# Rest tile in two units, paired partial sums and a new order of side tiles in a fused attention and feed-forward kernel

## The chip, the cores and the metric

One core of a Trainium2 chip. The metric is the device time of one execution in microseconds (us). Runs agree within 0.3%; all are fast, with a granted TensorE clock of 0.996 to 1.0.

## The reference

For each of four batches a set of 32 inducing rows attends to the 12416 tokens (phase 1, giving h), the tokens attend to h (phase 2), and a gated feed-forward layer follows.

```python
B, N, m, C = (4, 12416, 32, 128)          # n_tokens 49664, d_ff 1536
def mab(q, kv):
    s = scale * (q @ kv.transpose(0, 2, 1))
    a = np.exp(s - s.max(-1, keepdims=True))
    a /= a.sum(-1, keepdims=True) + 1e-09
    return a @ kv
h = mab(I, x)                              # phase 1: m x C per batch
x = mab(x, h)                              # phase 2
gate = np.maximum(x @ w_gate, 0.0); val = x @ w_val
out = gate * val @ w_out
```

## The kernel before

The product h x w_gate, h x w_val (called hgv) is made once per batch, so that gate and value of a token block come from matmuls of 32 rows. A batch has 97 tiles of 128 tokens: 12 pairs of 512-token blocks and one **rest tile**. A pair is 12 **units**, one for each 128 of the 1536 columns. The main loop takes one unit per **slot**:

```python
for k, ps in enumerate(unit["g"]):        # ScalarE: relu of two banks, one unit
    nc.scalar.activation(out=g16[:, k * BLK : (k + 1) * BLK], in_=ps, func=AF.Relu)
for a in range(0, n, w):                  # VectorE: gate * value, of an earlier unit
    nc.vector.tensor_tensor(out=ready["dst"][:, a : a + w],
        in0=ready["g16"][:, a : a + w], in1=ready["v"][:, a : a + w], op=ALU.mult)
```

Twelve output matmuls (a **chain**, six slots) sum a block in the one bank of kind "o"; ScalarE copies it out as oT. PSUM has three banks "g" (gates and all side work), two double banks "v" and one "o". Everything else is a **side tile**, put into a slot by a list of (first slot, last slot): the scores of phase 2 (p2, p2q), phase 1 of the next batch (p1T, the h parts with their copies hp and hq, z, hT), and hgv. A side tile is taken in the fifth slot of a chain:

```python
due = [f for f in fills if f[0] <= at]
late = min(due, key=lambda f: f[1])
if late[1] <= at:
    pick = late                            # its deadline is here: forced
elif not n_steps or job_slot == 5:
    pick = due[0]                          # the one that could start first
```

The rest tile was three units of 512 columns, in one gate bank each, and an h part summed 4 groups of tiles in one bank, seven times per batch:

```python
for s in range(3):
    yield dict(mm=[[(slice(i * P, (i + 1) * P), 4 * s + i, p2[r : r + 32, 0:P], hgv[r : r + 32, :])
                    for i in range(4)] for r in (0, 64)], ...)
def h_part(at, q):
    ps = bank("g", "h_ps", [P, P + 1])
    ...                                    # 4 + 16 matmuls of one part
    nc.scalar.copy(out=hq[0:n, :], in_=ps[0:n, :])
    nc.gpsimd.tensor_tensor(out=s["hp"][0:n, :], in0=s["hp"][0:n, :], in1=hq[0:n, :], op=ALU.add)
```

The softmax here doesn't subtract the row's maximum and nothing guards it: scores larger than these inputs give would overflow.

Of the kernel before, what the change touches and what calls it, by code (L numbers as in the profile page):

```python
# [18 lines left out]
def kernel(  # L19
# [16 lines left out]
    nc = tc.nc  # L36
# [302 lines left out]
    count = itertools.count()  # L339


    SPB = NPAIR * NFF + 3


    def slot(b, pr, s):
        if b == B - 1 and pr >= NPAIR - 1:
            return b * SPB + (NPAIR - 1) * NFF + (3 if pr < NPAIR else 0) + s
        return b * SPB + pr * NFF + s

    def order(b):  # L350
# [112 lines left out]
    for b in range(B):  # L463
        for qd in range(NPAIR // 2):
            base = slot(b, 2 * qd, 0)
            if base:

                a = base - 2 * NFF if qd else slot(b - 1, NPAIR, 0) - 14
                if b == B - 1 and qd == NPAIR // 2 - 1:

                    bl = 2 * NPAIR - 4
                    ev_s2(b, (b, 2 * qd), (bl, bl + 1, bl, bl + 1), a + 4, a + 8)
                    for k in range(2):
                        ev_s2(b, (b, 2 * qd + 1, k), (bl + 2 + k,) * 4, a + 16 + 6 * k, a + 20 + 6 * k)
                else:
                    ev_s2_quad(b, qd, a + (4 if a else 12), a + (8 if a else 18))
            else:
                ev_s2(b, (b, 1), (2, 3, 2, 3), 7, 8)
                ev_z2(lambda: p2s[(0, 0)], [(0, 0, k) for k in range(2)], TPB, 2)
        a = slot(b, NPAIR, 0)  # L480
        ev_s2_rest(b, a - 11, a - 4)


    def plan_phase1(b):
        s = state[b] = {}
        at0 = slot(b - 1, 0, 0)

        def begin():
            s["x16"] = new_x16()
# [4 lines left out]
        for q in range(NCH):  # L494
            t0, t1 = crange(q)

            def load(q=q):
                s["x32", q] = load_x(b, q)

            def cast(q=q, t0=t0, t1=t1):  # L500
                nc.gpsimd.tensor_copy(  # L501
                    out=s["x16"][:, t0:t1, :], in_=s["x32", q]
                )

            def transp(q=q, t0=t0, t1=t1):
                s["xT"][q] = new_xT(q)
                nc.sync.dma_start_transpose(
                    out=s["xT"][q],
                    in_=s["x16"][:, t0:t1, :].rearrange("p t c -> p (t c)"),
                )  # L510

            at = at0 + 14 * q if q < NQ else at0 + 7
            post[at + 3].append(load)
            post[at + 11].append(cast)
            post[at + 15].append(transp)

            def s1(at, q=q):
                fill(at + 9, at + 24, lambda at: h_part(at, q))
                ps = bank("g", "s1T_ps")
                for r in range(4):  # L520
                    t = q * CT + r * TPB
                    nc.tensor.matmul(
                        ps[32 * r : 32 * r + 32, :],
                        indT,
                        xTs(s["xT"], t, TPB),
                        start=True,
                        stop=True,
                    )

                def act():  # L530
                    p1T = st([P, BLK], FP16, "p1T", 3)
                    nc.scalar.activation(out=p1T, in_=ps, func=AF.Exp, scale=sm_scale)  # L532

                    def tr():
                        p1g = st([P, TPB, P], FP16, "p1g", NQ)
                        nc.sync.dma_start_transpose(out=p1g, in_=p1T)
                        s["p1g"][q] = p1g

                    post[at + 2].append(tr)

                post[at + 1].append(act)

            if q < NQ:
                fill(at + 22, at + 34, s1)

        at = at0 + 34

        def s1_rest(at):
            fill(at + 12, at + 24, lambda at: h_part(at, NQ))
            ps = bank("g", "s1T_ps")  # L550
            nc.tensor.matmul(ps[0:M, 0:P], indT, xTs(s["xT"], NT - 1, 1), start=True, stop=True)

            def act():
                p1T = st([P, BLK], FP16, "p1T", 3)
                nc.scalar.activation(
                    out=p1T[0:M, 0:P], in_=ps[0:M, 0:P], func=AF.Exp, scale=sm_scale
                )

                def tr():
                    p1r = st([P, 1, M], FP16, "p1r", 1)  # L560
                    nc.sync.dma_start_transpose(out=p1r, in_=p1T[0:M, 0:P])
                    s["p1r"] = p1r

                post[at + 2].append(tr)

            post[at + 1].append(act)

        fill(at, at + 6, s1_rest)

        def h_part(at, q):  # L570
            ps = bank("g", "h_ps", [P, P + 1])
            if q < NQ:
                n = P
                for t in range(TPB):
                    nc.tensor.matmul(
                        ps[:, P : P + 1],
                        s["p1g"][q][:, t, :],
                        ones16[:, 0:1],
                        start=(t == 0),
                        stop=(t == TPB - 1),  # L580
                    )
                for t in range(TPB):
                    for r in range(4):
                        nc.tensor.matmul(
                            ps[32 * r : 32 * r + 32, 0:P],
                            s["p1g"][q][:, t, 32 * r : 32 * r + 32],
                            s["x16"][:, q * CT + r * TPB + t, :],
                            start=(t == 0),
                            stop=(t == TPB - 1),
                        )  # L590
            else:
                n = M
                p1r = s["p1r"][:, 0, :]
                nc.tensor.matmul(ps[0:M, P : P + 1], p1r, ones16[:, 0:1], start=True, stop=True)
                nc.tensor.matmul(
                    ps[0:M, 0:P], p1r, s["x16"][:, NT - 1, :], start=True, stop=True
                )

            def act():
                if "hp" not in s:  # L600
# [1 line left out]
                    nc.scalar.copy(out=s["hp"], in_=ps)  # L602
                    return
                hq = st([P, P + 1], FP32, "hq", 2)
                nc.scalar.copy(out=hq[0:n, :], in_=ps[0:n, :])  # L605
                nc.gpsimd.tensor_tensor(  # L606
                    out=s["hp"][0:n, :], in0=s["hp"][0:n, :], in1=hq[0:n, :], op=ALU.add
                )
                if q == NQ - 1:
                    fill(at + 3, at + 8, z_join)  # L610

            post[at + 1].append(act)

# [1 line left out]
        def z_join(at):  # L615
# [16 lines left out]
                )  # L632

            post[at + 1].append(act)
            fill(at + 4, at + 8, h_join)

        def h_join(at):
            ps = bank("g", "hT_ps", [P, M])
# [2 lines left out]
            def act():  # L641
# [2 lines left out]
                    nc.scalar.copy(out=s["hT"][:, d * M : (d + 1) * M], in_=ps)  # L644
                s["hgv"] = new_hgv()
                for k in range(3):
                    ev_hgv(b, k, at + 2, at + 9 + 3 * k)

            post[at + 1].append(act)

# [4 lines left out]
    def chain(w, gv, key, k, t0, first):  # L655
# [46 lines left out]
            if key[0] == B - 1 and key[1] == NPAIR - 2:  # L702
                counts = (6, 5) if k == 0 else (4, 4)
        else:
            steps = [(first + i // 4, lambda i=i: step(i)) for i in range(NFF)]
            counts = ([4, 8], [4, 8])
        job(steps, evac, counts)

# [69 lines left out]
    def units():  # L778
        for b in range(B):
            for pr in order(b):  # L780
# [67 lines left out]
                else:  # L848
                    gvr = st([P, NFF, P], FP16, "gvr", 1)
                    chain(P, lambda i, g=gvr: g[:, i, :], (b, pr), 0, NT - 1, base + 4)  # L850
                    for s in range(3):
                        yield dict(
                            mm=[
                                [
                                    (
                                        slice(i * P, (i + 1) * P),
                                        4 * s + i,
                                        p2[r : r + 32, 0:P],
                                        hgv[r : r + 32, :],
                                    )  # L860
                                    for i in range(4)
                                ]
                                for r in (0, 64)
                            ],
                            dst=gvr[:, 4 * s : 4 * s + 4, :].rearrange("p i c -> p (i c)"),
                        )

    def form(ps, cols, s, p2, hgv):
# [1 line left out]

    def gate_banks(unit):

        n = unit["dst"].shape[-1] // BLK
        unit["g"] = [None] * n

        def gate(cols, s, p2, hgv):
            k, lo = divmod(cols.start, BLK)
# [19 lines left out]
    while True:  # L897
# [42 lines left out]
        if due:  # L940
            late = min(due, key=lambda f: f[1])
            if late[1] <= at:
                pick = late
            elif not n_steps or job_slot == 5:
                pick = due[0]
        if pick and n_steps > 1 and isinstance(c, int):
            if len(j["steps"]) - n_steps + 1 <= 3 * (c - job_slot):
                n_steps -= 1
# [13 lines left out]

        if unit:
            g16 = unit["g16"] = st([P, 2 * BLK], FP16, "g16", 4)
            for k, ps in enumerate(unit["g"]):
                nc.scalar.activation(out=g16[:, k * BLK : (k + 1) * BLK], in_=ps, func=AF.Relu)  # L966
        if ready:
            n = ready["dst"].shape[-1]
            w = n // ready.get("parts", 1)
            for a in range(0, n, w):  # L970
                nc.vector.tensor_tensor(  # L971
                    out=ready["dst"][:, a : a + w],
                    in0=ready["g16"][:, a : a + w],
                    in1=ready["v"][:, a : a + w],
                    op=ALU.mult,
                )
        at += 1

# [29 lines left out]
```

## Time and profile before

| | before |
|---|---|
| time, median | 708.68 us (708.39 to 709.48, 4 runs) |
| span of the profiled run | 706.6 us |
| VectorE, ScalarE, TensorE busy | 677.7, 676.1, 637.6 us |
| first multiplication begins, last one ends | 26.81, 702.56 us |
| multiplications' distances above the minimum | 16.6 us |
| TensorE's waits for oT at a chain's first matmul | 45.7 us, 94 times |

The multiplications' distances above the minimum are worked out from the single VectorE starts of the trace: the distance from one multiplication's start to the next, less 1.131 us for 1024 columns, 0.617 for 512, which are the shortest usual distances.

In the profile's lines, L971 is line 971 of the kernel; "gv<-g,v_ps" is the output and inputs by name; the bracket at the end of a line of the order in time is the engine's idle time ahead of it and what ended it. Line numbers move by up to 14 between the kernels: the multiplication is L971 before and L981 after, relu L966 and L969, the chain's matmuls L662 and L663.

### The profile page before, as it was taken

What the parts mean: (1) busy time and instruction counts of PE and PEld (TensorE: products, weight loads), DVE (VectorE), ACT (ScalarE), POOL (GpSimd) and SP (SyncE); (2) the same over time, 40 slices, a digit from 0 to 9 for tenths busy, and PEclk for the clock granted to TensorE, in tenths of its full rate; (3) what the DMA queues carried; (4) which work ended last, traced back from release to release, by engine and by line L of the source; (5) the groups of instructions that cost most, each with busy time, mean ns of one, the idle gap of its engine ahead of it and who ended that gap; (6) DMA issues with size and microseconds to landing.
All of it is one profiled execution on the core that took longest, in us unless ns stands there. A gap on an engine that the chain in (4) does not pass through costs nothing. (4 is left out here: it accounts for less than half of the span.)

```text
span 706.6 us, 14082 instructions
## 1 busy us (share of the span) xinstructions
PE 637.6 (90%) x4629; PEld 186.5 (26%) x4629; DVE 677.7 (96%) x619; ACT 676.1 (96%) x1384; POOL 350.4 (50%) x646
## 2 busy tenths in 40 slices
PE   6899999999988999999998999999999888888997
PEld 5422222222222222222222222222222222222224
DVE  4699999999999999999999999999999999999997
ACT  5799999999999999999999999999999999999996
POOL 3627636544275637356255472753516443534543
PEclk9999999999999999999999999999999999999999
DMA  8656666431258867523149666653223132231222
GB/s 342 219 137 178 161 169 165 109 94 47 84 141 166 201 162 215 118 77 84 53 88 218 169 171 167 165 120 81 63 68 93 50 90 59 78 90 50 71 58 89
DMA packets 142346, 87.58 MB, mean 124 GB/s; under 512 B 117152, under 2 KB 125632, under 8 KB 139968
## 3 DMA queue, kind: packets, MB, share of 16 engines
q1 hardware_dynamic: 142128, 86.62, 46.6%
q8 instruction: 36, 0.59, 0.4%
q14 instruction: 38, 0.31, 0.2%
q10 hardware_dynamic: 144, 0.07, 0.0%
HBM read 27.80 MB, written 25.43 MB: 75 GB/s over the span
## 5 line engine op out<-in xcount | busy, mean ns | idle before, releaser
L971 DVE TENSOR_TENSOR gv<-g,v_ps 128x1024 f16<-128x1024 f16 (+1 forms) x578 | 657.5, 1209 | 9.9 <-PE g_ps L869 6.0
L966 ACT ACTIVATE g<-g_ps 128x512 f16<-128x512 f32 x1164 | 604.2, 618 | 11.9 <-PE g_ps L869 8.4
L662 PE MATMUL o_ps<-gv,wo 128*128 128x512 f16 x1128 | 352.6, 384 | 43.9 <-ACT oT L668 43.9
L679 POOL TENSOR_SCALAR osb<-o,z2i 128x128 f32<-128x128 f16 x380 | 165.9, 452 | 280.5 <-DMA o<-oT 278.6
L869 PE MATMUL g_ps<-p,hgv 32*128 32x512 f16 x1152 | 284.1, 380 | 1.7 <-ACT g L966 1.0
L869 PE MATMUL v_ps<-p,hgv 32*128 32x512 f16 x1152 | 223.6, 383 | 8.7 <-DVE gv L971 6.9
L869 PEld LDWEIGHTS <-hgv 32*128 32x128 f16 x2400 | 69.8, 91 | 267.2 <-issue 263.1
L662 PEld LDWEIGHTS <-wo 128*128 128x128 f16 x1176 | 81.0, 97 | 212.3 <-issue 195.9
L430 POOL TENSOR_TENSOR z2i<-zt,minus 128x16 f32<-128x16 f32 (+3 forms) x31 | 73.2, 2365 | 0.3
L668 ACT CAST oT<-o_ps 128x512 f16<-128x512 f32 (+1 forms) x98 | 58.4, 596 | 0.1
L501 POOL CAST x<-x 128x2048 f16<-128x2048 f32 x18 | 34.0, 1890 | 14.1 <-DMA x<-in_x_dram 13.9
L423 POOL TENSOR_TENSOR zt<-zt 128x32 f32<-128x32 f32 (+5 forms) x124 | 35.1, 283 | 9.7
L423 POOL TENSOR_TENSOR zt<-p2T 128x256 f32<-128x256 f16 (+3 forms) x31 | 17.4, 562 | 24.3 <-DMA p2T<-p 14.0
L270 DVE COPY xT<-xT_ps 128x1024 f16<-128x1024 f16 (+1 forms) x13 | 8.4, 650 | 9.8 <-PE xT_ps L269 8.9
L269 PE MATMUL xT_ps<-eye,x 128*128 128x128 f16 x97 | 9.0, 242 | 5.2 <-POOL x L281 4.6
L282 ACT CAST x<-gv 128x512 f16<-128x512 f32 (+1 forms) x12 | 7.2, 597 | 6.8 <-DMA gv<-in_x_dram 6.8
L195 ACT ACTIVATE p2q<-s_ps 128x512 f16<-128x512 f32 x22 | 13.4, 611 | 0.0
L281 POOL CAST x<-gv 128x512 f16<-128x512 f32 (+1 forms) x12 | 7.2, 598 | 10.1 <-DMA gv<-in_x_dram 10.0
L532 ACT ACTIVATE p1T<-s1T_ps 128x512 f16<-128x512 f32 x18 | 11.1, 615 | 0.0
L179 PE MATMUL s_ps<-xT,hT 128*32 128x512 f16 x108 | 10.8, 389 | 0.1
L971 DVE TENSOR_TENSOR gvr<-g,v_ps 128x512 f16<-128x512 f16 x12 | 8.0, 685 | 1.7 <-PE g_ps L869 1.7
L606 POOL TENSOR_TENSOR hp<-hp,hq 128x129 f32<-128x129 f32 (+1 forms) x18 | 8.2, 458 | 2.5 <-ACT hq L605 2.5
(92 smaller groups left out, 159.5 us busy)
## 6 DMA issues: line engine op xcount, KB each, us to landing
out_dram<-osb SPq DMA_DIRECT2D x95, 256.0 KB, 2.2
x<-in_x_dram SPq DMA_DIRECT2D x18, 1024.0 KB, 5.6
gv<-in_x_dram SPq DMA_DIRECT2D x11, 512.0 KB, 7.4
p<-p2q SPq DMA_DIRECT2D x88, 64.0 KB, 2.0
o<-oT SPq DMA_TRANSPOSE x98, 2.4
x<-in_moe_w_out_dram SPq DMA_DIRECT2D x1, 768.0 KB, 9.1
gv<-in_x_dram SPq DMA_DIRECT2D x2, 256.0 KB, 10.3
x<-in_moe_w_gate_dram SPq DMA_DIRECT2D x1, 512.0 KB, 8.8
```

What stands on the lines that cost most here:

```text
L179: nc.tensor.matmul(ps[32 * r : 32 * r + 32, :], hT[:, 0:M], xTs(xT, blocks[r] * TPB, TPB), start=True, stop=True,)
L195: nc.scalar.activation(out=p2q, in_=ps, func=AF.Exp, scale=sm_scale)
L423: nc.gpsimd.tensor_tensor(out=dst, in0=v[:, :, :, 0:m], in1=v[:, :, :, m : 2 * m], op=ALU.add)
L430: nc.gpsimd.tensor_tensor(out=z2i, in0=v[:, :, :, 0], in1=minus1[:, 0 : n * g].rearrange("p (n g) -> p n g", n=n), op=ALU.pow,)
L501: nc.gpsimd.tensor_copy(out=s["x16"][:, t0:t1, :], in_=s["x32", q])
L532: nc.scalar.activation(out=p1T, in_=ps, func=AF.Exp, scale=sm_scale)
L662: nc.tensor.matmul(c["ps"][:, 0:w], wo[:, i, :], gv(i), start=(i == 0), stop=(i == NFF - 1))
L668: nc.scalar.copy(out=oT[:, 0:w], in_=c["ps"][:, 0:w])
L679: nc.gpsimd.tensor_scalar(out=osb[:, t, :], in0=o16[:, t, :], scalar1=zz, scalar2=zz, op0=ALU.mult, op1=ALU.mult,)
L869: nc.tensor.matmul(ps[:, cols], hgv[:, s * P : (s + 1) * P], p2, start=True, stop=True)
L966: nc.scalar.activation(out=g16[:, k * BLK : (k + 1) * BLK], in_=ps, func=AF.Relu)
L971: nc.vector.tensor_tensor(out=ready["dst"][:, a : a + w], in0=ready["g16"][:, a : a + w], in1=ready["v"][:, a : a + w], op=ALU.mult,)
```

## The change

The intent: fewer and fuller units for the rest tile, fewer ScalarE copies for the h parts, and side tiles spread evenly. The core of the diff:

```diff
-    SPB = NPAIR * NFF + 3
+    SPB = NPAIR * NFF + 2
 ...
-        a = slot(b, NPAIR, 0)
-        ev_s2_rest(b, a - 11, a - 4)
+        a = slot(b, 0, 0)
+        ev_s2_rest(b, a + 15, a + 45)
 ...
-        at0 = slot(b - 1, 0, 0)
+        at0 = slot(b - 1, 0, 0) - (12 if b > 1 else 0)
 ...
-                fill(at + 9, at + 24, lambda at: h_part(at, q))
+                if q % 2:
+                    fill(at + 9, at + 24, lambda at: h_part(at, (q - 1, q)))
 ...
-                fill(at + 22, at + 34, s1)
+                fill(at + 22, at + 38, s1)
 ... (h_part sums the tiles of two parts in one bank; the last also the rest tile, from a zeroed 128-column p1r)
-                    ev_hgv(b, k, at + 2, at + 9 + 3 * k)
+                    ev_hgv(b, k, at + 2, slot(b, 0, 0) - 2 + 4 * k)
 ...
-                    for s in range(3):
+                    for s in range(2):
                         yield dict(
                             mm=[[(
-                                        slice(i * P, (i + 1) * P),
-                                        4 * s + i,
+                                        slice(k * BLK + i * P, k * BLK + (i + 1) * P),
+                                        6 * s + 3 * k + i,
 ...                             # three 128-column pieces in each of two banks
-                pick = due[0]
+                pick = late
 ...
+            w = unit["dst"].shape[-1] // 2
             for k, ps in enumerate(unit["g"]):
                 nc.scalar.activation(
-                    out=g16[:, k * BLK : (k + 1) * BLK], in_=ps, func=AF.Relu
+                    out=g16[:, k * w : (k + 1) * w], in_=ps[:, 0:w], func=AF.Relu
 ...
```

More of the change, by code (lines that the diff above doesn't have):

```diff
@@ L339 @@
     count = itertools.count()
-    SPB = NPAIR * NFF + 3
+    SPB = NPAIR * NFF + 2
     def slot(b, pr, s):
         if b == B - 1 and pr >= NPAIR - 1:
-            return b * SPB + (NPAIR - 1) * NFF + (3 if pr < NPAIR else 0) + s
+            return b * SPB + (NPAIR - 1) * NFF + (2 if pr < NPAIR else 0) + s
         return b * SPB + pr * NFF + s
@@ L543, in plan_phase1 @@
             if q < NQ:
-                fill(at + 22, at + 34, s1)
+                fill(at + 22, at + 38, s1)
         at = at0 + 34
         def s1_rest(at):
-            fill(at + 12, at + 24, lambda at: h_part(at, NQ))
+            s["p1r"] = st([P, 1, P], FP16, "p1r", 1)
+            nc.gpsimd.memset(s["p1r"], 0.0)
             ps = bank("g", "s1T_ps")
@@ L559, in tr @@
                 def tr():
-                    p1r = st([P, 1, M], FP16, "p1r", 1)
-                    nc.sync.dma_start_transpose(out=p1r, in_=p1T[0:M, 0:P])
-                    s["p1r"] = p1r
+                    p1r = s["p1r"]
+                    nc.sync.dma_start_transpose(out=p1r[:, :, 0:M], in_=p1T[0:M, 0:P])
                 post[at + 2].append(tr)
             post[at + 1].append(act)
-        fill(at, at + 6, s1_rest)
-        def h_part(at, q):
+        fill(at + 0, at + 6, s1_rest)
@@ L571, in h_part @@
+        def h_part(at, qs):
             ps = bank("g", "h_ps", [P, P + 1])
-            if q < NQ:
-                n = P
-                for t in range(TPB):
-                    nc.tensor.matmul(
-                        ps[:, P : P + 1],
-                        s["p1g"][q][:, t, :],
-                        ones16[:, 0:1],
-                        start=(t == 0),
-                        stop=(t == TPB - 1),
-                    )
-                for t in range(TPB):
-                    for r in range(4):
-                        nc.tensor.matmul(
-                            ps[32 * r : 32 * r + 32, 0:P],
-                            s["p1g"][q][:, t, 32 * r : 32 * r + 32],
-                            s["x16"][:, q * CT + r * TPB + t, :],
-                            start=(t == 0),
-                            stop=(t == TPB - 1),
-                        )
-            else:
-                n = M
-                p1r = s["p1r"][:, 0, :]
-                nc.tensor.matmul(ps[0:M, P : P + 1], p1r, ones16[:, 0:1], start=True, stop=True)
+            tiles = [(q, t) for q in qs for t in range(TPB)]
+            rest = qs[-1] == NQ - 1
+            for q, t in tiles:
+                nc.tensor.matmul(
+                    ps[:, P : P + 1],
+                    s["p1g"][q][:, t, :],
+                    ones16[:, 0:1],
+                    start=(q, t) == tiles[0],
+                    stop=(q, t) == tiles[-1] and not rest,
+                )
+            if rest:
+                nc.tensor.matmul(
+                    ps[:, P : P + 1], s["p1r"][:, 0, :], ones16[:, 0:1], start=False, stop=True
+                )
+            for q, t in tiles:
+                for r in range(4):
+                    nc.tensor.matmul(
+                        ps[32 * r : 32 * r + 32, 0:P],
+                        s["p1g"][q][:, t, 32 * r : 32 * r + 32],
+                        s["x16"][:, q * CT + r * TPB + t, :],
+                        start=(q, t) == tiles[0],
+                        stop=(q, t) == tiles[-1] and not rest,
+                    )
+            if rest:
@@ L595, in h_part @@
                 nc.tensor.matmul(
-                    ps[0:M, 0:P], p1r, s["x16"][:, NT - 1, :], start=True, stop=True
+                    ps[:, 0:P], s["p1r"][:, 0, :], s["x16"][:, NT - 1, :], start=False, stop=True
                 )
@@ L604, in act @@
                 hq = st([P, P + 1], FP32, "hq", 2)
-                nc.scalar.copy(out=hq[0:n, :], in_=ps[0:n, :])
-                nc.gpsimd.tensor_tensor(
-                    out=s["hp"][0:n, :], in0=s["hp"][0:n, :], in1=hq[0:n, :], op=ALU.add
-                )
-                if q == NQ - 1:
-                    fill(at + 3, at + 8, z_join)
+                nc.scalar.copy(out=hq, in_=ps)
+                nc.gpsimd.tensor_tensor(out=s["hp"], in0=s["hp"], in1=hq, op=ALU.add)
+                if rest:
+                    fill(at + 3, at + 10, z_join)
             post[at + 1].append(act)
@@ L634, in z_join @@
             post[at + 1].append(act)
-            fill(at + 4, at + 8, h_join)
+            fill(at + 4, at + 10, h_join)
         def h_join(at):
@@ L704, in chain @@
         else:
-            steps = [(first + i // 4, lambda i=i: step(i)) for i in range(NFF)]
+            steps = [(first + i // 6, lambda i=i: step(i)) for i in range(NFF)]
             counts = ([4, 8], [4, 8])
@@ L860, in units @@
                                     )
-                                    for i in range(4)
+                                    for i in range(3)
+                                    for k, r in ((0, 64 * j), (1, 64 * j + 32))
                                 ]
-                                for r in (0, 64)
+                                for j in range(2)
                             ],
-                            dst=gvr[:, 4 * s : 4 * s + 4, :].rearrange("p i c -> p (i c)"),
+                            dst=gvr[:, 6 * s : 6 * s + 6, :].rearrange("p i c -> p (i c)"),
                         )
@@ L871, in gate_banks @@
     def gate_banks(unit):
-        n = unit["dst"].shape[-1] // BLK
-        unit["g"] = [None] * n
+        unit["g"] = [None] * 2
         def gate(cols, s, p2, hgv):
@@ L964 @@
             g16 = unit["g16"] = st([P, 2 * BLK], FP16, "g16", 4)
+            w = unit["dst"].shape[-1] // 2
             for k, ps in enumerate(unit["g"]):
-                nc.scalar.activation(out=g16[:, k * BLK : (k + 1) * BLK], in_=ps, func=AF.Relu)
+                nc.scalar.activation(
+                    out=g16[:, k * w : (k + 1) * w], in_=ps[:, 0:w], func=AF.Relu
+                )
         if ready:
-            n = ready["dst"].shape[-1]
-            w = n // ready.get("parts", 1)
-            for a in range(0, n, w):
+            w = ready["dst"].shape[-1] // 2
+            parts2 = ready.get("parts", 1)
+            dst, g16, v = (
+                t.rearrange("p (k c) -> p k c", k=2)
+                for t in (ready["dst"], ready["g16"][:, 0 : 2 * w], ready["v"])
+            )
+            for a in range(parts2):
+                ks = slice(a, a + 1) if parts2 == 2 else slice(0, 2)
                 nc.vector.tensor_tensor(
-                    out=ready["dst"][:, a : a + w],
-                    in0=ready["g16"][:, a : a + w],
-                    in1=ready["v"][:, a : a + w],
-                    op=ALU.mult,
+                    out=dst[:, ks, :], in0=g16[:, ks, :], in1=v[:, ks, 0:w], op=ALU.mult
                 )
```

## The prediction

> **What bounds the kernel now.** I read the busy totals first, then the list of instruction groups, then the order in time of each engine where its idle time lies. The page of the kernel before says:
>
> ```profile
> PE 637.6 (90%) x4629; PEld 186.5 (26%) x4629; DVE 677.7 (96%) x619; ACT 676.1 (96%) x1384; POOL 350.4 (50%) x646
> ...
> L971 DVE TENSOR_TENSOR gv<-g,v_ps 128x1024 f16<-128x1024 f16 (+1 forms) x578 | 657.5, 1209 | 9.9 <-PE g_ps L869 6.0
> L966 ACT ACTIVATE g<-g_ps 128x512 f16<-128x512 f32 x1164 | 604.2, 618 | 11.9 <-PE g_ps L869 8.4
> ```
>
> VectorE and ScalarE are both at 96%. The work is a stream of units: per unit ("slot") TensorE makes two gate banks and two value banks, ScalarE takes relu of the two gate banks, VectorE multiplies 128x1024. Everything else (phase 1 of the next batch, the evictions oT, the rest tile) is squeezed in between as "side tiles". VectorE's order in time shows where it is not back to back:
>
> ```profile
> 84.34 29.72 DVE L971 TENSOR_TENSOR gv<-g,v_ps 128x1024 f16<-128x1024 f16 x26 [0.42 <-PE g_ps L869]
> 114.74 73.02 DVE L971 TENSOR_TENSOR gv<-g,v_ps 128x1024 f16<-128x1024 f16 x64 [0.69 <-ACT p1T L532]
> 188.53 5.74 DVE L971 TENSOR_TENSOR gv<-g,v_ps 128x1024 f16<-128x1024 f16 x5 [0.78 <-PE g_ps L869]
> 194.20 1.31 DVE L971 TENSOR_TENSOR gvr<-g,v_ps 128x512 f16<-128x512 f16 x2
> 195.92 0.69 DVE L971 TENSOR_TENSOR gvr<-g,v_ps 128x512 f16<-128x512 f16 x1 [0.41 <-PE g_ps L869]
> 197.19 55.74 DVE L971 TENSOR_TENSOR gv<-g,v_ps 128x1024 f16<-128x1024 f16 x49 [0.58 <-PE g_ps L869]
> ```
>
> The columns are start, length, engine and group, and in brackets the idle time before it. Long stretches have no gap. One multiplication lasts 1.21 us, but the next starts 1.131 us after it (the commonest distance of the single starts in the trace; the 132 units after the third rest tile give (149.75-1.21)/131 = 1.134). So VectorE is the bound, and what can be gained is only its steps above 1.131 (for 512 columns 0.60). I summed these over all 590 multiplications: **17.1 us**. That is all there is to win, 2.4% of the time.
>
> ScalarE is nearly as full, and this decides where the steps get longer:
>
> ```profile
> 147.94 5.08 ACT L966 ACTIVATE g<-g_ps 128x512 f16<-128x512 f32 x10
> 152.90 0.28 ACT L605 COPY hq<-h_ps 128x129 f32<-128x129 f32 x1
> 153.43 1.08 ACT L966 ACTIVATE g<-g_ps 128x512 f16<-128x512 f32 x2 [0.25 <-PE g_ps L869]
> 154.40 0.59 ACT L668 CAST oT<-o_ps 128x512 f16<-128x512 f32 x1
> ```
>
> A relu every 0.477 to 0.494 us, so a slot costs ScalarE about 0.98. Six slots hold one oT (0.47): 12 x 0.489 + 0.47 = 6.34, against 6 x 1.131 = 6.79 for VectorE. One side tile more (0.48 to 0.53) makes 6.82 to 6.87. So **one side tile per six slots just fits**, at a loss of 66 to 90 ns of VectorE (the starts at 140.91, 147.77, 154.63, 161.51 are 6.86 to 6.88 apart), and a second one in the same six slots is lost nearly whole.
>
> The link that carries this to VectorE is on TensorE:
>
> ```profile
> 154.13 0.39 PE L869 MATMUL g_ps<-p,hgv 32*128 32x512 f16 x2
> 155.04 0.38 PE L662 MATMUL o_ps<-gv,wo 128*128 128x512 f16 x1 [0.52 <-ACT oT L668]
> 155.35 0.39 PE L869 MATMUL v_ps<-p,hgv 32*128 32x512 f16 x2
> ```
>
> There is one o bank. The next chain's first matmul waits for oT, everything behind it waits too, and the v_ps that VectorE needs comes 0.31 later.
>
> **What the Trainium skill says.** (1) "Perfetto Trace Analysis", section "Optimizing Scalar/DVE Operations": an operation pays about 60 ns (VectorE on SBUF, 125 on PSUM) or 51 ns (ScalarE on PSUM) beside its elements, and the profiled length is larger, since half of the access time overlaps the next instruction. The trace agrees for ScalarE: 0.477 = 512/1.2 + 50. For VectorE, with one operand in PSUM, 1.131 = 1024/0.96 + 64, the smaller figure. (2) "VectorE: DVE Perf Modes", section "Mode 1x (REGULAR) - the baseline": PSUM operands run at one result per cycle. The 1.131 agrees; nothing in the change alters it. (3) "TensorE: Matmul & The Clock Gate", Part 3: matmuls start and end in program order. The 0.52 wait above holding up v_ps agrees. (4) "TensorEngine Tiling (Array Packing)", "Column Tiling": matmuls into different column groups run in parallel. In the trace the 16 h matmuls start in fours 3 to 5 ns apart, a four every 45 to 56 ns.
>
> **The change, part by part.**
>
> *Where the 17.1 us lie*, each from the single VectorE starts: start-up (slots 1 to 12) 1.3; last pair 1.0; the four rest tiles 0.51 + 0.67 each, 4.7; places with two side tiles close together 6.4; the remaining 3.7 are the 40 to 90 ns of single side tiles. The crowded places are: two p1T two slots apart, about 0.64 to 0.70 in each of batches 0 to 2; h part and p1T two slots apart, 0.77, 0.34, 0.42; p2q in an odd slot, 0.35; p2q, hgv and the rest's scores before the batch boundary, 0.87, 0.75, 0.75; with after-effects 2.3, 2.2 and 1.9.
>
> *Rest tile.* Three units of 512 become two of 768. VectorE: 3 x 0.617 = 1.85 becomes 2 x (768/0.96 + 64 = 0.864) = 1.73, so -0.12 per batch, -0.5 in all (estimate from the trace's 1.131). ScalarE: 3 x 0.49 becomes 4 x (384/1.2 + 50 = 0.37), the same. The main effect: a short slot (0.617) had to hold the same 3 chain matmuls plus an oT as a long one. Now the slots are longer, there are two, the chain puts 2, 2 and 1 matmuls there, the recorded order shows no oT inside, and the scores are taken early in the batch. I expect 0.3 per batch to stay (in batch 1 an hgv tile falls there): 4 x (1.18 - 0.3) = -3.5.
>
> *Side tiles by deadline, phase 1 twelve slots ahead.* I built the changed kernel and read its ScalarE order: every side tile but the small z stands at the same place, one slot ahead of oT, one per six slots. So the crowded places go: -6.4. The tiles moved still cost their 66 to 90 ns: some 14 of them, +1.0.
>
> *h parts two at a time.* Per batch 7 copies become 3. ScalarE gets back 4 x 0.3 to 0.5; I put 4 single losses of about 50 ns, 3 batches: -0.6. But the matmuls of two parts now stand in one place on TensorE. A part took 152.13 to 152.64, 0.51: ones 4 x 25 ns, a change-over of 93, fours 3 x 50, a change-over of 152. A second part in the same place adds 4 x 25 + 4 x 50 = 0.30, the rest tile in the third some 0.15. TensorE is in order and had no slack there (its v_ps came just in time), so I take most of 0.3 + 0.3 + 0.45 per batch as VectorE time: 3 x 0.85 = +2.6.
>
> Sum: -0.5 - 3.5 - 6.4 + 1.0 - 0.6 + 2.6 = -7.4. I round it back to **-6.8**, since any wait inside a chain of three engines is added to by some new one: 708.8 - 6.8 = **702.0 us**, -1.0%. GpSimd (50% busy) gets fewer additions and one memset per batch, off the path. The tail: the last block's matmuls stand one slot later, but the last v_ps is no longer behind 20 of them; I count 0.
>
> **Rivals.** (a) *TensorE takes over at the double h parts.* For: 20 more matmuls in one slot, 90% busy. Against: only nine such places; at 0.8 us each it would eat 7 us, and the time would be 705 to 706. (b) *ScalarE becomes the bound*, as its side tiles now come in every group of six: 6.86 against 6.79 everywhere. Then all batches lose about 24 x 0.08 = 1.9, and the gain is 4 to 5: 704. For it: the measured 6.86 to 6.88. It is mostly in my sum. (c) *DMA.* Phase 1's loads and transposes start twelve slots earlier for batches 2 and 3, on top of the boundary. For: the DMA share is 0.8 where loads run. Against: the waits for DMA fall on GpSimd, which is half idle; oT has four buffers. The time would hardly move. (d) *Everything fits.* Double h parts hidden and rest tile at 0.86 per unit: 17.1 falls to about 7, 698 to 699.
>
> **Range and chances.** The centre is 702.0. Rival (d) gives the lower end with some slack, 699; (a) with (b) the upper end, 705.5. Faster by over 2% needs 694.7, that is 14.2 of the 17.1 us plus 0.5, while start-up, tail and single tiles alone hold 5: 3%. Slower by 2% needs a new wait of 21 us: 2%. The same within 2%: 95%.
>
> **What would show it.** In the changed profile: VectorE still steps 1.131; the steps above it sum to about 10; the rest tile shows two multiplications of 768 columns, 0.95 long, 0.86 apart, with under 0.3 idle after them; no gap of 0.4 or more at two close p1T, nor at hgv ahead of the boundary; a new loss of 0.3 to 0.5 at each of the nine h copies, with ScalarE idle 0.5 or more after hq. The prediction is wrong if the double h parts cost over 0.8 each or nothing, or if VectorE finds a new regular gap.

## The result, and the profile after

| | before | after |
|---|---|---|
| time, median | 708.68 us | 703.39 us (703.25 to 704.04, 4 runs) |
| span of the profiled run | 706.6 | 701.6 |
| first multiplication begins | 26.81 | 27.24 |
| last multiplication ends | 702.56 | 696.17 |
| from there to the end | 4.00 | 5.40 |
| distances above the minimum | 16.6 | 10.3 |

The ratio of after to before is 0.9925 (95% interval 0.9908 to 0.9943). A ratio is the mean time of one kernel's fast runs over that of the other's fast runs of the same rounds, so it is not quite the ratio of the two medians.

The page of the changed kernel, busy totals and the three groups that matter:

```profile
PE 632.8 (90%) x4629; PEld 183.8 (26%) x4629; DVE 676.7 (96%) x615; ACT 673.3 (96%) x1376; POOL 344.4 (49%) x637
...
L981 DVE TENSOR_TENSOR gv<-g,v_ps 128x1024 f16<-128x1024 f16 (+1 forms) x578 | 657.5, 1212 | 5.7 <-ACT g L969 1.9
L969 ACT ACTIVATE g<-g_ps 128x512 f16<-128x512 f32 (+1 forms) x1168 | 604.1, 619 | 7.4 <-PE g_ps L872 4.6
L663 PE MATMUL o_ps<-gv,wo 128*128 128x512 f16 x1128 | 352.2, 384 | 46.0 <-ACT oT L669 46.0
```

The same 96% and the same duration of a multiplication; what went is idle time. VectorE's order in time, after:

```profile
98.18 27.44 DVE L981 TENSOR_TENSOR gv<-g,v_ps 128x1024 f16<-128x1024 f16 x24 [0.21 <-PE g_ps L872]
125.80 27.58 DVE L981 TENSOR_TENSOR gv<-g,v_ps 128x1024 f16<-128x1024 f16 x24 [0.18 <-PE g_ps L872]
153.66 40.09 DVE L981 TENSOR_TENSOR gv<-g,v_ps 128x1024 f16<-128x1024 f16 x35 [0.28 <-PE g_ps L872]
193.68 1.81 DVE L981 TENSOR_TENSOR gvr<-g,v_ps 128x768 f16<-128x768 f16 x2
195.81 55.80 DVE L981 TENSOR_TENSOR gv<-g,v_ps 128x1024 f16<-128x1024 f16 x49 [0.32 <-ACT g L969]
```

The rest tile is one piece of two multiplications (the single ones are 0.95 long and 0.864 apart). The gaps of 0.69 at 114.74 and 0.78 at 188.53, which the prediction shows, are gone as gaps (at the second a step 0.23 too long stays). There are three new, smaller ones 27 us apart: the paired h parts. TensorE and ScalarE at the third of them:

```profile
151.93 0.34 PE L577 MATMUL h_ps<-ones,p1g 128*128 128x1 f16 x8
152.13 0.16 PE L585 MATMUL h_ps<-ones,p1r 128*128 128x1 f16 x1
152.22 0.63 PE L590 MATMUL h_ps<-x,p1g 128*32 128x128 f16 x32
152.79 0.23 PE L598 MATMUL h_ps<-x,p1r 128*128 128x128 f16 x1
152.85 0.38 PE L663 MATMUL o_ps<-gv,wo 128*128 128x512 f16 x1
```

```profile
153.05 0.27 ACT L608 COPY hq<-h_ps 128x129 f32<-128x129 f32 x1 [0.24 <-PE h_ps L598]
153.63 1.08 ACT L969 ACTIVATE g<-g_ps 128x512 f16<-128x512 f32 x2 [0.31 <-PE g_ps L872]
154.60 0.59 ACT L669 CAST oT<-o_ps 128x512 f16<-128x512 f32 x1
```

From 151.93 to the next chain matmul at 152.85 TensorE spends 0.92 us on the part (two parts and the rest tile's two matmuls), where a single one took 0.51. ScalarE waits 0.24 ahead of its copy and 0.31 after it.

The end of the program. TensorE's order in time before, then after:

```profile
699.20 1.29 PE L727 MATMUL o_ps<-wo,gv 128*128 128x128 f16 x20
700.42 0.39 PE L869 MATMUL v_ps<-p,hgv 32*128 32x512 f16 x2
700.75 1.68 PE L727 MATMUL o_ps<-wo,gv 128*128 128x128 f16 x24
702.62 0.40 PE L727 MATMUL o_ps<-wo,gv 128*128 128x128 f16 x4 [0.20 <-DVE gv L971]
```

```profile
693.49 0.62 PE L728 MATMUL o_ps<-wo,gv 128*128 128x128 f16 x8
694.04 0.39 PE L872 MATMUL v_ps<-p,hgv 32*128 32x512 f16 x2
694.36 2.85 PE L728 MATMUL o_ps<-wo,gv 128*128 128x128 f16 x48
```

Before, the last v_ps stood between 20 and 28 of the last block's 48 matmuls. After, all 48 follow it, to 697.21, while the last multiplication ends at 696.17. From that end to the issue of the last block's last store it is 1.67 us (1.08 before).

### The profile page after: what moved, and what is told of

It reads as the page before. It is cut to its first block, busy times and chain, and to the rows that moved or that the text cites. A ratio compares the mean times of both kernels' runs of the same rounds, so it can differ in the third digit from the quotient of the medians.

```text
span 701.6 us, 14033 instructions
## 1 busy us (share of the span) xinstructions
PE 632.8 (90%) x4629; PEld 183.8 (26%) x4629; DVE 676.7 (96%) x615; ACT 673.3 (96%) x1376; POOL 344.4 (49%) x637
## 4 chain that ended last, share of the span: by engine, by line
ACT 37%; PE 25%; issue 19%; DVE 13%; DMA 4%; POOL 1%; SPq 0%; ACTq 0%; POOLq 0%; DVEq 0%
ACT g L969 27%; DVE gv L981 13%; PE o_ps L663 11%; PE v_ps L872 8%; ACT oT L669 6%; PE g_ps L872 3%; DMA gv<-in_x_dram 2%; ACT p2q L195 2%; ACT p1T L533 2%; DMA xT<-x 1%; DMA o<-oT 1%; PE h_ps L590 1%; ACT hgv L170 1%; PE idle_ps L263 0%; POOL x L501 0%
## 5 line engine op out<-in xcount | busy, mean ns | idle before, releaser
L969 ACT ACTIVATE g<-g_ps 128x512 f16<-128x512 f32 (+1 forms) x1168 | 604.1, 619 | 7.4 <-PE g_ps L872 4.6
L872 PEld LDWEIGHTS <-hgv 32*128 32x128 f16 x2400 | 67.5, 91 | 268.2 <-issue 263.7
L195 ACT ACTIVATE p2q<-s_ps 128x512 f16<-128x512 f32 x22 | 13.4, 611 | 0.0
L292 ACT ACTIVATE p<-s_ps 128x256 f16<-128x256 f32 (+2 forms) x14 | 5.0, 354 | 3.9 <-PE s_ps L290 3.7
L269 PEld LDWEIGHTS <-x 128*128 128x128 f16 x97 | 6.8, 111 | 6.0 <-POOL x L281 5.5
```

The costliest lines, as they stand in the source:

```text
L195: nc.scalar.activation(out=p2q, in_=ps, func=AF.Exp, scale=sm_scale)
L269: nc.tensor.transpose(ps[:, t - t0, :], x16[:, t, :], eye16)
L872: nc.tensor.matmul(ps[:, cols], hgv[:, s * P : (s + 1) * P], p2, start=True, stop=True)
L969: nc.scalar.activation(out=g16[:, k * w : (k + 1) * w], in_=ps[:, 0:w], func=AF.Relu)
```

## The experiments

Twelve kernels ran, all with correct results, in five rounds; four or five executions of each count. Beside the time I give the **stretch**, from the start of the first multiplication to the end of the last (before 675.76, after 668.93), because the start-up differs from run to run: in these profiles the first multiplication began between 26.7 and 28.1 us, though all fourteen kernels run the same list of engine instructions ahead of it. Each stretch is of one profiled execution. How well it repeats can be read from the five kernels that have the same code through batches 0 to 2 (the changed one, the two with spare copies, the two that change the last batch alone): from the first multiplication to that of the third rest tile they take 501.14 to 501.21 us. So a difference of 0.1 in a stretch may be noise; those of 0.2 and more lie above it.

### Which part does it: rest tile, order, pairs

**Rest tile alone.** The kernel before with the rest tile in two units.

```diff
-    SPB = NPAIR * NFF + 3
+    SPB = NPAIR * NFF + 2
-                    for s in range(3):
+                    for s in range(2):      # and the six-piece form of the unit, relu and multiplication
```

> The kernel before with the rest tile in two units of 768 columns and nothing else of the change. My theory (each part saves its own steps of VectorE): 4 x (1.18 - 0.2) for the waits at the rest tile and 0.5 for the shorter work make -4.4; the last block's tail grows by 1.4 as in the changed kernel, so 705.7 us, and VectorE's steps above the minimum fall from 16.6 to about 12.7. Rival (the rest tile's waits come from the crowded side tiles around the boundary, hgv and oT): little is saved, 708 or more. Rival (the tail's growth comes from the side tiles' order): 704.3.

Measured: 706.27 us (706.02 to 706.39), stretch 672.36, end 5.06 us after the last multiplication. My theory but for its size: the stretch fell by 3.4, not 4.4, and the distances to 13.7, not 12.7. VectorE around the first rest tile of this kernel:

```profile
188.71 5.88 DVE L980 TENSOR_TENSOR gv<-g,v_ps 128x1024 f16<-128x1024 f16 x5 [0.78 <-PE g_ps L871]
194.51 1.86 DVE L980 TENSOR_TENSOR gvr<-g,v_ps 128x768 f16<-128x768 f16 x2
196.55 3.63 DVE L980 TENSOR_TENSOR gv<-g,v_ps 128x1024 f16<-128x1024 f16 x3 [0.18 <-PE g_ps L871]
```

The gaps of 0.41 and 0.58 inside and after the rest tile are one of 0.18, while the 0.78 of the crowded side tiles ahead of it stands as before. So the rest tile's waits were its own, and the longer end comes with the rest tile too, not with the order of side tiles.

**Order alone.** The kernel before with deadlines, the lead and the early rest scores; h parts single, rest tile in three units.

```diff
-                pick = due[0]
+                pick = late
-        ev_s2_rest(b, a - 11, a - 4)
+        ev_s2_rest(b, slot(b, 0, 0) + 15, slot(b, 0, 0) + 45)
-        at0 = slot(b - 1, 0, 0)
+        at0 = slot(b - 1, 0, 0) - (12 if b > 1 else 0)    # and the wider windows
```

> The kernel before with the scheduling alone (deadlines, phase 1 twelve slots ahead, rest scores early); rest tile in three units, h parts one at a time. My theory: the 6.4 us of crowded places go, 1.0 is paid for the tiles moved, and two crowded places per batch remain since there are 26 side tiles for 24 groups of six (6 x 0.45 = 2.7): -2.7, 706.0 us. Rest tile still with two waits, 0.5 and 0.67, tail 4.0. Rival (scheduling needs the pairing to do anything): 708. Rival (it is the whole of the gain): 703.5.

Measured: 707.88 us (707.77 to 708.75), stretch 675.06, only 0.7 less than before; the end 3.99. A miss by 1.9. Two things kept the gain. The crowded places remained in number: I find eight losses of 0.39 to 0.75 where two side tiles stand close (for example hq and p1T two slots apart at 153.3, 0.60). And an hgv tile now fell inside the short slots of the rest tile in each of batches 0 to 2: these cost 0.20 + 0.47 + 0.67 instead of 0.49 + 0.65.

**All but the pairs.** The changed kernel with single h parts.

```diff
-                if q % 2:
-                    fill(at + 9, at + 24, lambda at: h_part(at, (q - 1, q)))
+                fill(at + 9, at + 24, lambda at: h_part(at, q))   # and the rest tile's part apart
```

> The changed kernel with the h parts one at a time again, the rest tile's part apart, the rest kept. My theory: a double part costs VectorE some 0.32 more than a single one, 9 x 0.32 = 2.9 is saved; four more side tiles per batch find no free group of six for two of them per batch, 6 x 0.45 = 2.7 plus 6 x 0.07 are lost; so about 703.6 us, the same as the changed kernel within 0.5. Rival (the pairing is what makes room, as intended): 706 or more. Rival (the pairing only costs): 701.

Measured: 704.93 us (704.87 to 705.11), stretch 670.85, that is 1.9 worse than the changed kernel. The truth lies between my theory and the rival: pairing is worth 1.9 net, although each pair costs what I said.

**Rest tile and pairs, without the order.**

```diff
-                pick = late
+                pick = due[0]
-        at0 = slot(b - 1, 0, 0) - (12 if b > 1 else 0)
+        at0 = slot(b - 1, 0, 0)              # and the old windows, rest scores late
```

> The changed kernel without its scheduling part (earliest start instead of deadline, no lead of twelve slots, rest scores late, the old windows): the kernel before plus rest tile in two units plus h parts in pairs. In the recorded order of ScalarE each of batches 0 to 2 has two p1T two slots apart, and hgv, p2q and the rest's scores within four slots ahead of the boundary. My theory (both parts are needed together): 3 x (0.45 + 0.8) more than the changed kernel, 707.0 us, worse than the rest tile alone (706.3), since the double parts are paid and nothing is got for them. Rival (fewer side tiles make room in any order): 704.

Measured: 706.34 us (706.26 to 707.03), stretch 672.60. Not better than the rest tile alone (672.36), as the theory says, though 0.7 less bad. VectorE in this kernel:

```profile
132.88 20.57 DVE L981 TENSOR_TENSOR gv<-g,v_ps 128x1024 f16<-128x1024 f16 x18 [0.43 <-PE g_ps L872]
...
187.46 1.22 DVE L981 TENSOR_TENSOR gv<-g,v_ps 128x1024 f16<-128x1024 f16 x1 [0.34 <-PE g_ps L872]
189.19 5.74 DVE L981 TENSOR_TENSOR gv<-g,v_ps 128x1024 f16<-128x1024 f16 x5 [0.51 <-PE g_ps L872]
```

The first gap is two p1T two slots apart, the others hgv, p2q and the rest's scores within four slots. The five stretches together:

| stretch in us | h parts single | h parts in pairs |
|---|---|---|
| rest tile in three units, old order | 675.76 (before) | not run |
| rest tile in three units, new order | 675.06 | not run |
| rest tile in two units, old order | 672.36 | 672.60 |
| rest tile in two units, new order | 670.85 | 668.93 (after) |

With the rest tile in two units, order alone brings 1.5, pairs alone cost 0.2, both bring 3.4. **They need each other**: a batch has 24 groups of six slots; unpaired, 26 side tiles want a place (6 p2q, 7 p1T, the rest's scores, 7 h copies, z, hT, 3 hgv), and paired in the old order they still meet.

### Two parts of the order, one at a time

**No lead of twelve slots.**

```diff
-        at0 = slot(b - 1, 0, 0) - (12 if b > 1 else 0)
+        at0 = slot(b - 1, 0, 0)
```

> The changed kernel with phase 1 of batches 2 and 3 not twelve slots ahead. My theory: the side tiles still stand one per six slots, with one hgv tile just behind the boundary in each batch as in batch 1 of the changed kernel, where the boundary costs VectorE 0.7 and not 0.14 to 0.2: 2 x 0.5 = +1.0, 704.4 us. Rival (the lead is what makes room): a crowded place or more per batch, 706. Rival (earlier loads collide with the boundary's transfers): faster, 702.5.

Measured: 703.82 us (703.1 to 704.38), stretch 669.02, against 668.93, a difference of the size of the noise: the lead is worth nothing here. What I expected at the boundary is there (0.40 + 0.08 in batches 1 and 2, where the changed kernel has 0.14), but it is made up for elsewhere in the batch. The rival about transfers is not supported either.

**Earliest start instead of deadline.**

```diff
-                pick = late
+                pick = due[0]
```

> The changed kernel with side tiles taken by the earliest start again, not by the deadline. In the recorded order of ScalarE only two places per boundary differ (hgv comes before p2q, which is forced two slots behind it). My theory: p2q four slots after hgv costs 0.2 to 0.4 in each of two batches, 704.0 us. Rival (taking by deadline is the main part): 706 or more.

Measured: 703.69 us (703.27 to 704.25), stretch 669.63, 0.7 more. My theory in the stretch (0.4 to 0.8); in the time it is within the scatter.

### Does one side tile per six slots fit, and not a second?

A spare ScalarE copy in the last batch, in twelve groups of six slots without a side tile; then two of them.

```diff
+        rel = at - slot(B - 1, 0, 0) - 3
+        if 4 <= rel // 6 < 20 and rel // 6 % 4 != 1 and rel % 6 in (0,):      # second kernel: (0, 3)
+            nc.scalar.copy(out=st([P, BLK], FP16, "spare", 1), in_=wg[:, 0:BLK])
```

> The changed kernel with a spare ScalarE copy (128x512, to a tile that nobody reads) in each of twelve groups of six slots of the last batch that have no side tile, at the place of a side tile, one slot ahead of oT. My theory (one side tile per six slots just fits): 12 x 0.07 = +0.8 us, 704.2. Rival (ScalarE is full, any work counts whole): 12 x 0.5 = +6, 709.4. Rival (VectorE alone is the bound, ScalarE has slack of several per cent): 703.4.

> As with one spare copy, but a second one three slots later in each of the twelve groups. My theory (the second in a group of six is lost whole): 12 x (0.07 + 0.5) = +6.8 us, 710.2, so that one copy and two copies differ by about 6. Rival (VectorE alone is the bound): below 704.5. Rival (any work counts whole): +12, 715.

Measured: one copy 704.87 us (704.68 to 704.89), two copies 710.94 us (710.82 to 711.93), against 703.39. The first set costs 1.5: ten times 0.083 to 0.086, once less than 0.06, and 0.57 once, where I had overlooked that the last batch's own scores stand close. The second set costs 6.1 more, 0.51 each. VectorE in the last batch with one copy, then with two:

```profile
569.66 71.09 DVE L984 TENSOR_TENSOR gv<-g,v_ps 128x1024 f16<-128x1024 f16 x62
```

```profile
582.62 6.97 DVE L984 TENSOR_TENSOR gv<-g,v_ps 128x1024 f16<-128x1024 f16 x6 [0.41 <-PE g_ps L872]
590.01 4.71 DVE L984 TENSOR_TENSOR gv<-g,v_ps 128x1024 f16<-128x1024 f16 x4 [0.41 <-PE g_ps L872]
```

With one copy 62 multiplications run without a gap; with two, a gap of 0.41 follows a pair of copies. Both rivals are ruled out: ScalarE is neither slack nor fully bound. VectorE's 6.79 us for six slots leave ScalarE room for one tile besides oT, and for no other.

### Where the side tile stands

A chain's first matmul waits about 0.5 us for oT (47.9 us in all). I put the side tile's matmuls ahead of that matmul instead of into the fifth slot.

```diff
-            elif not n_steps or job_slot == 5:
+            elif not n_steps or job_slot == 1:
+        if pick and job_slot == 1:
+            fills.remove(pick)
+            pick[3](at)
+            pick = None
```

> The changed kernel with each side tile put ahead of a chain's first matmul, which waits 0.5 us for oT, instead of into the chain's fifth slot. My theory (a side tile costs VectorE what it adds to TensorE and ScalarE between relu and that wait): TensorE now makes the side tile's matmuls while it would wait, so the 0.29 + 0.12 of each of nine double h parts falls to about 0.1, and ScalarE's extra work comes after oT and no longer delays it: some 20 losses of 0.07 go down: -2.5 to -3.5, 700.4 us. Rival (ScalarE's sum over six slots, 6.82 to 6.87 against 6.79, is the limit wherever the tile stands): the 0.07 stay, only the h parts gain: 701.3. Rival (a bank of gates is held longer): no gain, 703.4.

Measured: 700.28 us (700.19 to 701.01), stretch 666.37, distances above the minimum 7.7. The ratio to before is 0.9883 (0.987 to 0.9897). TensorE at the third h part, and then TensorE's waits for oT in the changed kernel and in this one (us in total, times, longest):

```profile
146.94 0.63 PE L590 MATMUL h_ps<-x,p1g 128*32 128x128 f16 x32
147.51 0.23 PE L598 MATMUL h_ps<-x,p1r 128*128 128x128 f16 x1
147.57 0.38 PE L663 MATMUL o_ps<-gv,wo 128*128 128x512 f16 x1
```

```profile
PE o_ps L663 <- ACT oT L669: 47.9, 97, 0.6
```

```profile
PE o_ps L663 <- ACT oT L669: 13.4, 30, 0.6
```

The chain's matmul after the h part no longer waits, the waits fell from 97 to 30 (this view leaves out waits under 0.15 us, and most of the others are now about 0.07; TensorE's whole idle time, its span less its busy time, fell from 68.8 to 48.3), and the third h part of a batch costs VectorE 0.12 instead of 0.29 to 0.49; at the first two no step is above 0.06. Of the single tiles 25 losses of over 60 ns stay, as the rival for them said, so that half of my theory failed. The edit moves a pair's copy too, behind oT; but a single h part, with the same copy in the old place, costs 0.09 or less in 18 of 21 cases of the kernel before (the other 3 have a p1T close by), and a pair 0.29 to 0.49. So the cost of a pair was its longer time on TensorE between two relus, not its copy. Of the 3.1 us gained, 2.6 are in the stretch; 0.4 of the rest are at the end (5.03 instead of 5.40), which I did not look into.

### The end of the program

The scale of the last block's output, zz, is made by GpSimd. **Rest chain of the last batch in one slot**, so that the last block starts a slot earlier:

```diff
-            counts = ([4, 8], [4, 8])
+            counts = ([4, 8], [4, 8]) if key[0] < B - 1 else ([12], [12])
```

> The changed kernel with the twelve small matmuls of the last batch's rest chain in one slot instead of two. My theory: the time from VectorE's last multiplication to the end grew from 4.0 to 5.4 us because the last block's first half ends a slot later and leaves all 48 matmuls of the second half after the last v_ps; this puts 20 of them back ahead of it, so the end comes 1.4 us after less: 702.0 us, with 4.0 us after the last multiplication. Rival (it is GpSimd's zz that came late, behind four scalings): 703.3, zz still ends last. Rival (the tail differs from run to run): 703.4.

Measured: 702.88 us (702.64 to 703.53), end 4.70 after the last multiplication instead of 5.40, stretch 669.20. From the last multiplication's end to the issue of the last store it is 1.08 again. So 0.59 of the longer end are the 48 matmuls; a step of 0.41 was added where the twelve stood together.

**The last block faster, and zz early.**

```diff
-                        job(steps, evac, ([1, 3, 3, 3, 3] if k == 0 else [5] * 8,) * 2)
+                        job(steps, evac, ([1, 3, 4, 4] if k == 0 else [5] * 8,) * 2)
+            zz[0] = st([P, TPB, 1], FP32, "zz", 1)     # moved ahead of the four scalings
```

> The changed kernel with the last block's first half stepping 1, 3, 4, 4 instead of 1, 3, 3, 3, 2, so that it ends a slot earlier, and with GpSimd's zz ahead of its four scalings. Putting the rest chain into one slot moved the end by 0.7 only, because 0.3 was lost where twelve small matmuls stood together. My theory: from VectorE's last multiplication to the end 5.4 falls to 4.2, two slots with four steps cost 0.1 each: 702.4 us. Rival (GpSimd's zz ended last): zz alone explains it, DVE's last idle time is then no longer put down to it and the end is 4.4 or less. Rival (nothing): 703.4.

Measured: 703.02 us (702.83 to 703.3), end 4.58, last store again 1.08 after the last multiplication; the stretch grew to 669.62, more than expected. No gain worth having, and zz was not needed to explain the end: it was early in this kernel and late in the one before, with the same 1.08.

**All together.** Side tiles first, the second p2q of a batch two slots earlier, the rest chain in one slot, zz early.

```diff
-                    ev_s2_quad(b, qd, a + (4 if a else 12), a + (8 if a else 18))
+                    ev_s2_quad(b, qd, a + ((2 if qd == 1 else 4) if a else 12), a + (8 if a else 18))
```

> Side tiles ahead of the chain's first matmul, as in the run before (700.3), with three small things more: the second p2q of each batch two slots earlier (so that it no longer stands beside the rest tile's oT and a p1T; that cost VectorE 0.14 + 0.21 in two batches), the last rest chain in one slot, and zz ahead of the four scalings. My theory: -0.7 for p2q, -0.5 for the tail, as measured in the changed kernel (703.4 to 702.9): 699.1 us, VectorE's steps above the minimum at 7.3 or less. Rival (these small places are made up for elsewhere): 700.3.

Measured: 700.86 us (700.3 to 701.06), stretch 667.01: no better than 700.28. The p2q in its new place costs 0.39 beside the rest tile's oT in each of three batches, where it had cost 0.14 + 0.21 in two. The rival was right. The best version is the one before it, **700.28 us**, which beats both kernels.

## Why the prediction was right, point by point

- **The time.** Predicted 702.0 (699.0 to 705.5), measured 703.39: inside. The gain in the stretch was predicted as 6.8 and is 6.83 (675.76 to 668.93; 0.5 of it is the rest tile's shorter work, 6.3 the distances). That they agree to 0.03 is luck: the terms made 7.4, 0.6 was taken off without a term of its own, and it is the rest tile that came 0.6 short. The rest of the difference lies outside it: 1.4 at the end, 0.4 at the start, which is chance.
- **VectorE is the bound, and its distances above the minimum are all there is.** Right: multiplications still follow 1.131 apart, the sum fell to 10.3 ("about 10" was predicted).
- **One side tile per six slots just fits.** Right, and shown directly by the spare copies: 0.08 for the first, 0.51 for the second.
- **Rest tile.** Predicted 4.0 (3.5 + 0.5); alone it brought 3.4. Of the 0.6, 0.2 was counted twice: 12 multiplications are taken at 0.60 in the 3.5 and at 0.617 in the 0.5. What stays in the changed kernel is 0.48, 0.14, 0.14 and 0.26, where 0.3 each was said.
- **Double h parts.** Predicted 2.6 for nine. The losses in the changed kernel are 0.41, 0.38, 0.49, then 0.41, 0.41, 0.29, then 0.38, 0.41, 0.29, in sum 3.4; less 9 x 0.09 for single parts that is 2.6. Right. (That different column groups work in parallel, point (4) of the prediction, stands in the cited page under "Key Properties".)
- **Side tiles by deadline: -6.4 + 1.0, and pairs: -0.6 + 2.6.** The sum, -3.4, is what both bring together (672.36 to 668.93, also 3.4). How I split it was wrong. I read the spread-out places from the finished kernel and booked all of them to the order. Alone the order brings 0.7, or 1.5 beside the new rest tile; the pairs, which I booked as a cost, make the room for it. The lead of twelve slots brings nothing, the choice by deadline 0.7.
- **"The tail ... I count 0."** The mis-sized term: it is 1.4. I had set against the later 48 matmuls that the last v_ps comes earlier. It does (0.87 after the one before it, not 1.54), but VectorE was not what the end waited for: 48 matmuls from 694.36 take until 697.21. That is 0.59 to the last store's issue, shown by three kernels that put 20 of them back and have 1.08 again. The other 0.8 lie between that issue and the end: 2.92 before and with the order alone, 3.4 to 4.1 in the kernels with the two-unit rest tile, whether or not the last block was mended. The trace's landing times place them in the last block's last store itself: from issue to landing it takes 2.03 us before and 2.04 with the order alone, 2.85 in the changed kernel, and 2.4 to 3.2 in all kernels with the two-unit rest tile. Why it lands later is open; that earlier stores are still under way closer to it is only an argument.
- **The signs.** VectorE's losses at the h copies were as said. Two signs missed in size: after the first rest tile VectorE is idle 0.32 (under 0.3 was said), and ScalarE is idle 0.31 after the third hq (0.5 or more was said), besides 0.24 ahead of it.
- **Rivals.** (a) TensorE's h parts cost 0.4 each and not 0.8. (b) ScalarE's 0.07 to 0.09 per group is there and was in the sum. (c) Nothing of the transfers shows. (d) did not come in this form; with the side tiles in another place the distances fell to 7.7.

Open besides: two steps of 0.42 and 0.39 above the minimum at 259.9 and 406.2 us of the changed kernel, with no crowd of side tiles near. The kernel before has one of 0.35 at nearly the same multiplication as the first; the kernel with side tiles first has none.

## What to carry to other kernels

Where a full engine's work comes in equal steps, sum the distances of its starts above the shortest one and list where they lie: the list prices each part of a change, and its total says what no change can exceed that leaves the engine's own work as it is. Count what the second-fullest engine can take per period of the first, and give every period the same load; a tile too many in one period is lost whole (0.51 here), a free period elsewhere does not pay it back. Put extra work of an in-order engine just ahead of an instruction that will wait anyway: this alone, without any work removed, brought 3.1 us here, 2.6 of them in the stretch.

## What the Trainium skill lacked or had wrong

- "Perfetto Trace Analysis", "Optimizing Scalar/DVE Operations": gives about 125 ns of overhead for VectorE on PSUM. A multiplication with one operand in PSUM and the output in SBUF steps 64 ns above its elements at 0.96 GHz, for 1024 columns (1.131 us) and for 768 (0.864 us); the 267 ns between the two are 256 elements at that rate.
- "ScalarE: Activation LUTs", "What ACT_TABLE_LOAD costs": 186 ns + 0.833 N and an overlap of 93 ns make 520 ns from start to start for 512 columns. Relus that read PSUM start as little as 477 ns apart here, which agrees with the 51 ns of the prediction's point (1). The formula for one alone gives 613; the trace shows 591 to 735, three quarters of them up to 640.
- "TensorEngine Tiling (Array Packing)", "Key Properties": says that changing the tiling mode drains TensorE, without a number. Here a 512-column matmul that follows one of its kind starts 215 to 227 ns after it, and a matmul of 32 rows mostly 308 to 323 ns after it, so a change in this direction costs about 90 ns.
- No page says where in an in-order stream to place work that has slack. Moving the same matmuls ahead of a waiting one cut TensorE's waits of over 0.15 us for oT from 47.9 to 13.4 us, its whole idle time from 68.8 to 48.3 us, and the time from 703.4 to 700.3 us.
